# A semaphore wait from each indirect scatter to the eviction of the step ahead of it

## The chip, the cores and the metric

The kernel runs on one core of one Trainium2 chip. The metric is the device time of one execution in microseconds, the median over several runs. In the profile PE is TensorE, PEld its weight loads, DVE is VectorE, ACT is ScalarE, POOL is GpSimd, and SP is SyncE, which issues most of the DMAs. A "q" behind an engine's name means its sequencer.

## The reference

Four sequences of 10048 rows with 128 channels go through a long convolution (by FFT in the reference) with a filter that a small network makes from position embeddings. Each row of the result then goes to one of 16 experts, which are chosen in two stages (a group, then an expert within it).

```python
h_filt = (np.maximum(pos_emb @ w1, 0.0) @ w2) * np.exp(-0.01 * pos)[:, None]
u = x * v
y = np.fft.irfft(np.fft.rfft(u, n=2*S, axis=1) * np.fft.rfft(h_filt, n=2*S, axis=0)[None], n=2*S, axis=1)[:, :S]
a = x * y                                   # 4 x 10048 x 128, then seen as 40192 rows
g = np.argmax(a @ w_group, axis=1)          # group, and its softmax weight
e = np.argmax(a @ w_expert[g], axis=1)      # expert in the group, and its weight
out = g_w * e_w * (np.maximum(a @ moe_w1[g, e], 0.0) @ moe_w2[g, e])
```

## The kernel before

The program has two parts: `conv`, and behind it `moe`. The convolution is a two-step discrete Fourier transform by matmuls. The loop `for b in range(self.nbat + 1)` in `conv` handles one sequence per round, in two phases that follow one another.

**The forward phase** of round b has 43 steps of three channels (GD = 3). A step multiplies x by v (`product`, L434, on DVE, from an `xv` load that SP issues at L431), folds the product into sums and differences (`fold`: L447 on DVE or POOL, L448 on POOL for b > 1), takes the first transform on PE (`dft_blocks`, L387), and evicts it from PSUM into the large buffer `z` (L392, a copy on ACT for every b > 0). `run_ahead` is called first in each step: the product is traced four steps ahead of the transform and the fold three steps ahead. Loads have five buffers (NLOAD), folded products five (NPROD). A load's buffer is free when both halves of its fold are done. For b > 0 the inverse transform of the round before is woven into the same steps: transposes of `z` on PE (`turned`, L648 and L658) with a copy on ACT (tt, L660), then for every second step a group of matmuls (`inverse_blocks`, L683 and L691), two copies on ACT (oo, L700 and L701), and on DVE an addition (yt, L704) and a product (xy, L706) with `xo`, whose load ACT's own queue issues (L671).

**The middle phase** has 40 iterations, two frequencies in each. PE makes `psb` (L458), DVE the products t (L616, L619), POOL sums and differences of these into y (L617, L620), and, four iterations later, PE transforms back (`back`, L628) and ACT evicts into `z` (L635). The last round (b = 4) has only the inverse of the last sequence.

**Routing and scatters.** After a sequence is through, `chosen` and `ranked` pick experts and compute for every row an address among pages of 256 rows, one expert to a page. The rows themselves go there by indirect DMAs of POOL: `put` (L353) scatters one block of 128 rows with 130 columns out of a staged tile (`stg`, which SP loads and whose last two columns POOL fills in at L345), and `clear` (L368) marks the unused rows of pages. They wait in a list, and `scatter(n)` takes up to n of them: one or two in each forward step, after `run_ahead` and before that step's `dft_blocks`; one in three of four middle iterations, behind `back`; one or two in each step of the last round, behind `inverse_blocks`; the rest in `moe`, where `fetch` calls it.

**Order.** A planner orders each engine's instructions by a model of times, with program order as the priority. `keep_in_program_order` ties an instruction behind the one traced before it on its engine, without a semaphore. `between` does that for a scatter and also ties it behind the last instruction passed to `beyond`; `beyond` ties its instruction (L345, L448 for b > 1, L620, the part of L706 on POOL) behind all scatters since. So on POOL a scatter of a forward step stands in front of the next step's L448, and a scatter of a middle iteration in front of the next L620.

Of the kernel before, what the change touches and what calls it, by code (L numbers as in the profile page):

```python
# [139 lines left out]
class Kernel:  # L140
# [5 lines left out]
    def emit(self):  # L146
        tc, nc, d = self.tc, self.nc, self.d
        with ExitStack() as ctx:
            cp = ctx.enter_context(tc.tile_pool(name="const", bufs=1))
            self.ident = cp.tile([128, 128], F32, name="ident")  # L150
            make_identity(nc, self.ident)
            st = ctx.enter_context(tc.tile_pool(name="state", bufs=1))
            self.rem = st.tile([128, NE], F32, name="rem")
            self.cur = st.tile([128, NE], F32, name="cur")
            self.used = st.tile([128, 1], F32, name="used")
            for t in (self.rem, self.cur, self.used):
                nc.vector.memset(t, 0.0)
            pg = self.pages
            pg.epg = st.tile([128, pg.hp], F32, name="epg")
            pg.epgi = [st.tile([1, hi - lo], I32, name=f"epgi{lo}") for lo, hi in pg.parts]  # L160
            pg.count = st.tile([1, 1], I32, name="count")
            nc.vector.memset(pg.epg, 0.0)
            self.entries = ctx.enter_context(tc.tile_pool(name="entries", bufs=2))
            self.empty = st.tile([128, ZR, RW], F32, name="empty")
            nc.vector.memset(self.empty, 0.0)
            nc.vector.memset(self.empty[:, :, 128], BIGID)
            self.units, self.staged, self.tick, self.sent = [], 0, 0, None
            self.all = [Page(self, q) for q in range(pg.n)]
            self.w = [None, None]
            with ExitStack() as right:  # L170
                rout = ExitStack()
                self.rp = rout.enter_context(tc.tile_pool(name="rout", bufs=1, reuse_waits="tile"))
                with ExitStack() as c2:
                    routing = self.conv(c2, right)
                with ExitStack() as c2:
                    self.moe(c2, right, routing)
                rout.close()
# [131 lines left out]
    def scatter(self, n):  # L309
        self.tick += 1  # L310
        for _ in range(min(n, len(self.scatters))):
            b, send, tick, u = self.scatters[0]
            if u:
                self.stage(u.k)

            if tick > self.tick and n < NB:
                break
            self.between(send())
            self.scatters.pop(0)

    def unordered(self, ins, group, *others):
# [57 lines left out]
    def dft_blocks(self, b, eo, d0, n, other=False):  # L379

        nc = self.nc
        pool, tag = (self.psA, "ps") if b not in ("h", 0) or d0 // GD % 2 else (self.psT, "pt")
        ps = pool.tile([128, GD, 2 * NB], F32, tag=tag, name="psa")
        for i in range(n):

            for h, hs in enumerate(HALVES):
                nc.tensor.matmul(  # L387
                    ps[hs, i], eo[:, i, hs], self.fa[:, h], start=True, stop=True
                )
        copy = nc.vector.tensor_copy if other else nc.scalar.copy  # L390

        ins = copy(  # L392
            self.z[:, :NB, :, d0 : d0 + n].rearrange("p k s d -> p (k s) d"),
            ps[:, :n].rearrange("p d c -> p c d"),
        )
        self.in_turn(b, ins)
        self.tc.declare_no_dep(ins.ins, group=f"z{b}", reason="every step has channels of its own")
        self.tc.add_to_no_dep_group(f"z{b}", ins.ins)
# [224 lines left out]
    def back(self, k0, n, bp, y):  # L623

        nc = self.nc
        po = self.psT.tile([128, 2, 2, 128], F32, tag="pt", name="pbp")
        for i in range(n):
            nc.tensor.matmul(  # L628
                po[:, i].rearrange("p s d -> p (s d)"),
                bp[:, i],  # L630
                y[:, i].rearrange("p s d -> p (s d)"),
                start=True,
                stop=True,
            )
        nc.scalar.copy(self.z[:, k0 : k0 + n], po[:, :n])  # L635

    def turned(self, d0, n):

# [25 lines left out]
    def inverse_blocks(self, b, xy, d0, n, tts):  # L664

        nc, d, sp = self.nc, self.d, self.sp
        rows = lambda t: t[:, : n * NB].rearrange("p (t d) -> p t d", d=n)
        xo = sp.tile([128, GI * NB], F32, tag="spec", name="xo", bufs=NSPEC)
        src = d["x_out"][b, :, d0 * NB : (d0 + n) * NB]
        if b < self.nbat - 1:  # L670
            nc.scalar.dma_start(xo[:, : n * NB], src)  # L671
        else:
            self.tc.keep_in_program_order(nc.sync.dma_start(xo[:, : n * NB], src))
        po = self.psO.tile([128, GI, NB], F32, tag="po", name="po")
        c0 = d0 % (2 * GI)

        for c in range(c0, c0 + n):


            if c == c0 or c % 4 == 0:  # L680
                g, m = c // 4, min(4 - c % 4, c0 + n - c)
                for h, hs in enumerate(HALVES):
                    nc.tensor.matmul(  # L683
                        po[hs, c - c0 : c - c0 + m].rearrange("p c t -> p (c t)"),
                        tts[0][:, g, hs],
                        self.fi[:, h, 1 + c % 4 : 1 + c % 4 + m].rearrange("p c t -> p (c t)"),
                        start=c == c0,
                        stop=False,
                    )
            for h, hs in enumerate(HALVES):  # L690
                nc.tensor.matmul(  # L691
                    po[hs, c - c0],
                    tts[1 + c // 4][:, c % 4, hs],
                    self.fi[:, h, 0],
                    start=False,
                    stop=c == c0 + n - 1,
                )
        oo = rows(sp.tile([128, GI * NB], F32, tag="oo", name="oo"))
        by_row = po[:, :n].rearrange("p d t -> p t d")
        nc.scalar.activation(oo[0:64], by_row[64:128], AF.Copy, scale=-1.0)  # L700
        nc.scalar.copy(oo[64:128], by_row[0:64])  # L701
        pool, tag, bufs = (self.ap, "y", NY) if b < self.nbat - 1 else (sp, "yt", 2)
        yt = rows(pool.tile([128, GI * NB], F32, tag=tag, name="yt", bufs=bufs))
        nc.vector.tensor_tensor(yt, by_row, oo, ALU.add)  # L704
        helped = b == self.nbat - 1 and d0 // GI % 2 > 0
        ins = (nc.gpsimd if helped else nc.vector).tensor_tensor(  # L706
            xy[:, :, d0 : d0 + n], yt, rows(xo), ALU.mult
        )
        if helped:
            self.beyond(ins)  # L710
# [311 lines left out]
    def moe(self, ctx, right, routing):  # L1022
        tc, nc = self.tc, self.nc
        pools = [
            right.enter_context(tc.tile_pool(name=n, bufs=b, side="right", reuse_waits="tile"))
            for n, b in (("moe", 2),)
        ]
        self.sp = pools[0]
        self.psx = ctx.enter_context(tc.tile_pool(name="psx", bufs=1, space=PSUM, reuse_waits="tile"))
        self.psh = ctx.enter_context(tc.tile_pool(name="psh", bufs=4, space=PSUM, reuse_waits="tile"))  # L1030
        self.psy = ctx.enter_context(tc.tile_pool(name="psy", bufs=2, space=PSUM, reuse_waits="tile"))
        self.pst = ctx.enter_context(tc.tile_pool(name="pst", bufs=1, space=PSUM, reuse_waits="tile"))
        self.psr = lambda shape, name: self.pst.tile(shape, F32, tag="pt", name=name)
        pg = self.pages
        self.routing, self.fix = routing, tc.keep_in_program_order
        self.outs, self.spare, self.owed, self.part = [], 0.0, 0.0, 0.0
        self.work(self.all[: pg.usual])
        if pg.usual < pg.n:
            count = self.sp.tile([1, 1], I32, tag="ep", name="count", bufs=3)
            tc.keep_in_program_order(nc.vector.tensor_copy(count, pg.count))  # L1040
            count = nc.values_load(count, min_val=0, max_val=pg.n)
            self.rest(count, pg.usual)
# [366 lines left out]
```

## Time and profile before

| | us |
|---|---|
| median of 3 runs | 2088.56 |
| lowest, highest | 2079.05, 2088.92 |
| the profiled execution | 2083.55 |
| its span, first to last instruction | 2081.7 |
| PE busy in the span | 1963.7 |
| POOL busy | 1393.3 |
| mean granted TensorE clock | 0.973 |

The span is the time from the first to the last instruction that the profile shows; the execution's own time has 1.85 us more around it. The convolution takes about the first 1010 us. Its first scatter starts at 448.8 us: rounds b = 0 and 1 have none in front of that. Their forward phases with scatters lie at 487 to 587 us (b = 2) and 737 to 827 us (b = 3), the middle phases behind these at 587 to 684 and 827 to 927 us, and the last round from there to about 1010 us.

### The profile page before, as it was taken

To read this page: it belongs to the slowest core of one execution; us is meant where nothing else is said; L and a number is where in the kernel's file an instruction comes from. 1 tells how busy PE (TensorE), PEld (TensorE's weight loads), DVE (VectorE), ACT (ScalarE), POOL (GpSimd) and SP (SyncE) were. 2 spreads that over 40 slices of the span, in tenths; PEclk is the share of its full clock that TensorE was granted. 3 is DMA by queue.
4 is the path that set the end of the run, shared out by engine and by line. 5 is a ranking of instruction groups with operands and counts; after the bars stand their busy time and mean duration, and the time that the engine had idled before them with its cause. 6 is when DMAs were issued, how large, how long until landed. Compare 5 with 4: busy or idle time off the path is not lost.

```text
span 2081.7 us, 53885 instructions
## 1 busy us (share of the span) xinstructions
PE 1963.7 (94%) x18062; PEld 1803.7 (87%) x18062; DVE 1635.2 (79%) x3451; ACT 1408.2 (68%) x3081; POOL 1393.3 (67%) x1481
## 2 busy tenths in 40 slices
PE   8988999988899788989899999999999999999997
PEld 7867888777787577768699999999999999999997
DVE  5587775797558865696698998889999998888885
ACT  6652376435553355436688788888888888888886
POOL 3157600677889888976457677888888886555554
PEclk9999999998999789999999999999999999999999
DMA  4699866976799567968544455555555544443442
GB/s 136 227 264 257 282 178 189 326 208 176 207 308 297 168 186 223 326 225 278 187 130 138 134 154 151 155 178 171 156 161 155 162 149 131 125 135 120 127 126 66
DMA packets 258719, 388.92 MB, mean 187 GB/s; under 512 B 32679, under 2 KB 132626, under 8 KB 258432
## 3 DMA queue, kind: packets, MB, share of 16 engines
q1 hardware_dynamic: 225024, 318.01, 51.0%
q0 software_dynamic: 23904, 51.83, 7.0%
q10 hardware_dynamic: 9504, 15.54, 2.7%
q8 instruction: 146, 2.39, 0.5%
q14 instruction: 141, 1.16, 0.2%
HBM read 303.24 MB, written 83.04 MB: 186 GB/s over the span
## 4 chain that ended last, share of the span: by engine, by line
PE 66%; POOL 10%; DVE 8%; DMA 7%; issue 6%; ACT 2%; SPq 0%; POOLq 0%; ACTq 0%; DVEq 0%
PE py L1278 7%; PE ph L1259 7%; PE ph L1257 7%; PE py L1276 7%; PE py L1277 7%; PE ph L1258 7%; PE psb L458 4%; PE psa L387 4%; PE pbp L628 3%; POOL prow L353 3%; DMA xv<-xv_in 2%; PE ptm L1290 2%; PE px L1214 2%; PE pt L658 2%; PE po L683 1%
## 5 line engine op out<-in xcount | busy, mean ns | idle before, releaser
L1266 DVE SCALAR_TENSOR_TENSOR hl<-ph,hh 128x512 fp32r<-128x512 f32 x656 | 445.1, 683 | 93.0 <-ACT hh L1265 92.2
L1265 ACT ACTIVATE hh<-ph 128x512 fp32r<-128x512 f32 x656 | 393.8, 600 | 137.9 <-PE ph L1259 75.0
L1302 POOL DMA_INDIRECT out<-os,to x328 | 347.2, 1058 | 91.5 <-issue 71.4
L353 POOL DMA_INDIRECT prow<-stg,adr x316 | 350.4, 1109 | 73.0 <-issue 54.1
L1276 PE MATMUL py<-hh,wh 128*128 128x256 f32 x1312 | 398.5, 304 | 0.0
L1278 PE MATMUL py<-hh,wl 128*128 128x256 f32 x1312 | 373.1, 284 | 5.4 <-POOL wl L1246 5.4
L1257 PE MATMUL ph<-xh,wh 128*128 128x256 f32 x1312 | 373.4, 285 | 4.3 <-ACT wh L1239 2.5
L1259 PE MATMUL ph<-xh,wl 128*128 128x256 f32 x1312 | 373.4, 285 | 0.4 <-DVE wl L1246 0.4
L1258 PE MATMUL ph<-xl,wh 128*128 128x256 f32 x1312 | 372.8, 284 | 0.0
L1277 PE MATMUL py<-hl,wh 128*128 128x256 f32 x1312 | 371.3, 283 | 0.0
L1246 POOL TENSOR_TENSOR wl<-ws,wh 128x512 fp32r<-128x512 f32 x162 | 220.0, 1358 | 201.3 <-ACT wh L1239 200.3
L1278 PEld LDWEIGHTS py<-hh,wl 128*128 128x128 f32 x1312 | 251.3, 192 | 8.2 <-POOL wl L1246 8.2
L1257 PEld LDWEIGHTS ph<-xh,wh 128*128 128x128 f32 x1312 | 252.7, 193 | 5.0 <-ACT wh L1239 2.7
L1259 PEld LDWEIGHTS ph<-xh,wl 128*128 128x128 f32 x1312 | 253.0, 193 | 1.1 <-DVE wl L1246 0.8
L1258 PEld LDWEIGHTS ph<-xl,wh 128*128 128x128 f32 x1312 | 253.1, 193 | 0.1
L1277 PEld LDWEIGHTS py<-hl,wh 128*128 128x128 f32 x1312 | 252.7, 193 | 0.0
L1276 PEld LDWEIGHTS py<-hh,wh 128*128 128x128 f32 x1312 | 251.9, 192 | 0.0
L635 ACT COPY z<-pbp 128x512 f32<-128x512 f32 (+1 forms) x160 | 92.6, 580 | 221.8 <-PE pbp L628 214.9
L1246 DVE TENSOR_TENSOR wl<-mw,wh 128x512 fp32r<-128x512 f32 x328 | 236.6, 722 | 0.0
L617 POOL TENSOR_TENSOR y<-t 128x256 f32<-128x256 f32 (+1 forms) x160 | 120.3, 752 | 158.3 <-DVE t L616 153.0
L458 PE MATMUL psb<-z,bt 128*128 128x256 f32 x790 | 203.0, 389 | 10.5 <-DVE hs L591 3.7
L1239 ACT CAST wh<-mw 128x512 fp32r x328 | 205.7, 628 | 0.0
(232 smaller groups left out, 4367.4 us busy)
## 6 DMA issues: line engine op xcount, KB each, us to landing
ws<-m_w SPq DMA_DIRECT2D x328, 256.0 KB
ht<-hspec SPq DMA_DIRECT2D x156, 256.0 KB
xv<-xv_in SPq DMA_DIRECT2D x131, 288.0 KB
bt<-c_b SPq DMA_DIRECT2D x95, 256.0 KB
xg<-prow SPq DMA_DIRECT2D x164, 130.0 KB
bp<-c_bp SPq DMA_DIRECT2D x76, 256.0 KB
stg<-xyd SPq DMA_DIRECT2D x76, 256.0 KB
xyd<-xy SPq DMA_DIRECT2D x57, 256.0 KB
```

The lines of the kernel that those rows point to most:

```text
L353: ins = self.nc.gpsimd.indirect_dma_start(self.d["prow"], bass.IndirectOffsetOnAxis(ap=u.adr[:, t : t + 1], axis=0), u.rows[:, t - u.t0], ...
L458: nc.tensor.matmul(ps[:, i], bt[:, i], self.z[:, k0 + i], start=True, stop=True,)
L1246: ins = v.tensor_tensor(lo, self.matrix(i, half, self.ed), self.wh[i][half].bitcast(F32), ALU.subtract)
L1257: k.fix(nc.tensor.matmul(ph[:, j], wh, self.xh, start=True, stop=False))
L1258: k.fix(nc.tensor.matmul(ph[:, j], wh, self.xl, start=False, stop=False))
L1259: k.fix(nc.tensor.matmul(ph[:, j], wl, self.xh, start=False, stop=True))
L1265: k.fix(nc.scalar.activation(hh, ph, AF.Relu))
L1266: k.fix(nc.vector.scalar_tensor_tensor(hl, ph, 0.0, hh.bitcast(F32), ALU.max, ALU.subtract))
L1276: k.fix(nc.tensor.matmul(self.py, wh, self.hh[c], start=(c == 0), stop=False))
L1277: k.fix(nc.tensor.matmul(self.py, wh, self.hl[c], start=False, stop=False))
L1278: k.fix(nc.tensor.matmul(self.py, wl, self.hh[c], start=False, stop=(c == NC - 1)))
L1302: ins = k.nc.gpsimd.indirect_dma_start(k.d["out"], bass.IndirectOffsetOnAxis(ap=self.to[:, h : h + 1], axis=0), o[:, h], None, bounds_chec ...
```

## The change

A field `pace` keeps the instruction that evicted last. It is set by the eviction of each forward step (L392), of each `back` (L635), and in the last round by the second copy of each inverse group (L701). Each scatter that `scatter` sends while `pace` is set gets a dependency on it of the class that makes a semaphore wait. In a forward step that is the eviction of the step before, since the scatter is traced before its own step's `dft_blocks`; in a middle iteration it is the eviction of the `back` traced just in front of it; in the last round that of the group just traced. Before `moe` sends scatters, `pace` is set to None, so those get no such wait.

```diff
@@ emit
-            self.units, self.staged, self.tick, self.sent = [], 0, 0, None
+            self.units, self.staged, self.tick, self.sent, self.pace = [], 0, 0, None, None
@@ scatter
-            self.between(send())
+            ins = send()
+            self.between(ins)
+            if self.pace is not None:
+                kind = mybir.DependencyInfo(mybir.DependencyClass.Sync, mybir.DependencyReason.DATA)
+                self.tc.add_manual_dep(ins.ins, self.pace.ins.name, kind, reason="one step at a time")
             self.scatters.pop(0)
@@ dft_blocks
+        self.pace = ins
         self.in_turn(b, ins)
@@ back
-        nc.scalar.copy(self.z[:, k0 : k0 + n], po[:, :n])
+        self.pace = nc.scalar.copy(self.z[:, k0 : k0 + n], po[:, :n])
@@ inverse_blocks
-        nc.scalar.copy(oo[64:128], by_row[0:64])
+        ins = nc.scalar.copy(oo[64:128], by_row[0:64])
+        if b == self.nbat - 1:
+            self.pace = ins
@@ moe
-        self.routing, self.fix = routing, tc.keep_in_program_order
+        self.routing, self.fix, self.pace = routing, tc.keep_in_program_order, None
```

## Rows read from the trace of the kernel before

**Rows 1.** The page: busy time of each engine, its share of the span, and its count of instructions.

```profile
PE 1963.7 (94%) x18062; PEld 1803.7 (87%) x18062; DVE 1635.2 (79%) x3451; ACT 1408.2 (68%) x3081; POOL 1393.3 (67%) x1481
```

**Rows 2.** Busy time of the engines in the four stretches, the two forward phases with scatters first, then the middle phases behind them: from:to, length, busy us and count of each engine, granted clock, share of the DMA engines, GB/s.

```profile
487.00:587.00 100.00, 90.50 (x1286) 79.01 (x1286) 55.71 (x99) 61.70 (x109) 81.62 (x93) 0.95 0.77 211
737.00:827.00 90.00, 81.71 (x1140) 71.36 (x1132) 47.83 (x100) 54.35 (x97) 73.43 (x84) 0.92 0.75 211
587.00:684.00 97.00, 89.61 (x567) 69.95 (x565) 78.80 (x154) 38.46 (x89) 89.40 (x113) 1.00 0.92 307
827.00:927.00 100.00, 91.85 (x571) 72.17 (x569) 79.44 (x169) 39.15 (x90) 91.36 (x117) 0.98 0.82 276
```

**Rows 3.** The chain that ended last within 487 to 587 us: its shares by line.

```profile
by line: issue 28.7%; POOL prow L353 21.9%; POOL eo L448 10.9%; DMA xv<-xv_in 8.0%; PE psa L387 5.2%; DMA prow<-stg,adr 4.6%; PE pt L658 3.2%; PE po L683 2.9%; PE po L691 2.7%; ACT oo L700 1.8%; DVE eo L447 1.8%; DVE xv L434 1.7%; ACT oo L7
```

**Rows 4.** The scatter's line L353: all of its scatters, those of the first forward phase with the semaphore instructions of POOL's sequencer at that line, and those of the second forward phase; count, ns min/median/max, first and last start in us.

```profile
L353 POOL DMA_INDIRECT prow<-stg,adr x316: 966/998/1835, 487.5 to 1706.0; - x158
...
L353 POOL DMA_INDIRECT prow<-stg,adr x50: 966/1004/1656, 487.5 to 585.1; - x50
...
L353 POOLq EVENT_SEMAPHORE  x11: 42/43/43, 507.9 to 578.3; - x11
...
L353 POOL DMA_INDIRECT prow<-stg,adr x46: 966/1000/1814, 738.0 to 823.4; - x46
```

**Rows 5.** The timeline of POOL: start, duration in us, line, and in brackets how long the engine was idle before and who ended that.

```profile
487.55 1.03 POOL L353 DMA_INDIRECT prow<-stg,adr  x1 [0.68 <-POOL stg L345]
...
494.81 0.75 POOL L448 TENSOR_TENSOR eo<-xv 96x192 f32<-96x192 f32 x1 [3.60 <-PE psa L387]
...
537.16 1.65 POOL L353 DMA_INDIRECT prow<-stg,adr  x1 [0.16 <-issue]
...
587.85 0.89 POOL L617 TENSOR_TENSOR y<-t 128x256 f32<-128x256 f32 x1 [1.74 <-DVE t L616]
...
600.31 0.99 POOL L353 DMA_INDIRECT prow<-stg,adr  x1 [0.16 <-issue]
...
797.58 0.61 POOL L448 TENSOR_TENSOR eo<-xv 96x192 f32<-96x192 f32 x1
...
803.53 0.61 POOL L448 TENSOR_TENSOR eo<-xv 96x192 f32<-96x192 f32 x1
...
823.40 0.97 POOL L353 DMA_INDIRECT prow<-stg,adr  x1 [0.30 <-issue]
...
827.88 0.89 POOL L617 TENSOR_TENSOR y<-t 128x256 f32<-128x256 f32 x1 [3.51 <-DVE t L616]
...
927.29 0.99 POOL L353 DMA_INDIRECT prow<-stg,adr  x1 [0.17 <-POOL y L620]
...
937.64 1.37 POOL L706 TENSOR_TENSOR z<-yt,xo 128x474 f32<-128x474 f32 x1 [9.35 <-DVE yt L704]
```

**Rows 6.** The timeline of ACT, in the same columns; the row at 824.27 holds the evictions of the last two steps.

```profile
491.09 0.55 ACT L392 COPY z<-psa 128x474 f32<-128x474 f32 x1
...
522.83 0.56 ACT L700 ACTIVATE oo<-po 64x474 f32<-64x474 f32 x1 [3.78 <-DVE eo L447]
...
593.61 0.58 ACT L635 COPY z<-pbp 128x512 f32<-128x512 f32 x1 [1.97 <-PE pbp L628]
...
824.27 1.01 ACT L392 COPY z<-psa 128x474 f32<-128x474 f32 x2
...
933.75 0.55 ACT L701 COPY oo<-po 64x474 f32<-64x474 f32 x1
```

**Rows 7.** Who waited for whom: us in total, times, longest us. The first three rows are of 487 to 587 us, the last two of 737 to 827 us.

```profile
DVE xv L434 <- DMA xv<-xv_in: 16.4, 12, 2.7
...
PE pt L658 <- ACT tt L660: 9.5, 5, 2.9
...
POOL eo L448 <- PE psa L387: 6.5, 5, 3.6
...
PE pt L658 <- ACT tt L660: 8.3, 4, 3.1
...
POOL eo L448 <- PE psa L387: 3.2, 4, 1.7
```

**Rows 8.** The timeline of DVE, in the same columns.

```profile
518.94 0.71 DVE L434 TENSOR_TENSOR xv<-xv 96x384 f32<-96x384 f32 x1 [2.34 <-DMA xv<-xv_in]
...
521.72 0.64 DVE L706 TENSOR_TENSOR xy<-yt,xo 128x474 f32<-128x474 f32 x1
...
537.30 0.64 DVE L706 TENSOR_TENSOR xy<-yt,xo 128x474 f32<-128x474 f32 x1
...
806.75 0.42 DVE L434 TENSOR_TENSOR xv<-xv 96x256 f32<-96x256 f32 x1 [0.75 <-DMA xv<-xv_in]
```

**Rows 9.** The timeline of PE, in the same columns.

```profile
524.96 0.85 PE L658 MATMUL pt<-ident,z 128*128 128x128 f32 x4 [2.06 <-ACT tt L660]
...
803.91 0.98 PE L387 MATMUL psa<-fa,eo 96*64 96x158 f32 x12
```

**Rows 10.** The timeline of SP's queue, in the same columns.

```profile
804.16 0.31 SPq L431 DMA_DIRECT2D xv<-xv_in  x1
```

**Rows 11.** The product L706 on DVE in the first and in the second forward phase: count, ns min/median/max, first and last start.

```profile
L706 DVE TENSOR_TENSOR xy<-yt,xo x19: 487/642/654, 488.8 to 584.8; 128x474 f32<-128x474 f32 x18, 128x316 f32<-128x316 f32 x1
...
L706 DVE TENSOR_TENSOR xy<-yt,xo x16: 488/642/873, 740.8 to 824.8; 128x474 f32<-128x474 f32 x15, 128x316 f32<-128x316 f32 x1
```

## The prediction

> **What bounds the kernel now.** I read the page first: PE is busy 94% of the span, POOL 67% [rows 1]. An average like that hides the stages, so next come the four stretches of the convolution in which POOL scatters [rows 2]. There POOL is busy 82 of 100, 73 of 90, 89 of 97 and 91 of 100 us. The reader is to see that POOL has almost no room just where the change adds a wait; each scatter costs about 1.00 us of it (median 1.00, longest 1.81 in these phases), and there are 50 and 46 in the two forward phases [rows 4]. The chain of waits in the first of these phases confirms it: the scatter and the fold behind it have 33% of it, the xv loads that the fold sets free 8% [rows 3]. PE is nearly as full, and what it loses there is 9.5 and 8.3 us of waiting for the copy tt on ACT [rows 7].
>
> The decisive view is the pairing of scatters with the evictions they would wait for. I counted both off the loops in the order in which they are traced, and took the start of the k-th scatter and the end of its eviction from the timelines. 204 scatters come while `pace` is set (180 of L353, 24 of L368); the other 136 of the 316 [rows 4], and 8 of L368, fall in `moe` and get nothing.
>
> **The change part by part.**
>
> *Middle phases, 60 scatters.* Here the eviction is over long before. The first pair: eviction 593.61 + 0.58 = 594.19, scatter 600.31, so 6.1 us to spare [rows 5, 6]. Over all 60 the margin is 2.1 us or more. The wait is already met: 0 us. That matters, since POOL is at its fullest here.
>
> *Last round, 33 scatters.* One stands ahead of its eviction: it starts at 927.29, the eviction ends at 933.75 + 0.55 = 934.30, 7.0 us later. POOL's next work starts at 937.64 after 9.35 us of idling [rows 5, 6], so the scatter, moved to 934.4 to 935.4, still fits: 0 us. The others have 1 us or more to spare.
>
> *Forward phases, 111 scatters.* 64 of them start before their eviction ends, by 90.9 us together. The first of the 64 starts at 487.55 against 491.64 (491.09 + 0.55), 4.1 us early; the last at 823.40 against 825.00, where the first of the two copies in the row at 824.27 ends [rows 5, 6]. The 90.9 us don't add up, because POOL works in order: once the first scatter has waited, everything behind it is late too, and the following ones wait only for what is left. I moved POOL's rows accordingly, each only as far as its eviction or its predecessor pushes it, and left the evictions where they are. The folds L448 then come 2.4 us later on average in the first phase and 2.2 us in the second (4.2 and 3.8 us at most). Idle time of POOL, such as the 3.60 us in front of the L448 at 494.81 [rows 5], takes up a part early on.
>
> What is behind a waiting scatter on POOL: the L448 of a step four further on, and by it two consumers. The first is PE's transform. The shortest lead of a finished fold over its transform in either phase behind the first scatters is 797.58 + 0.61 = 798.19 to 803.91, 5.7 us [rows 5, 9]; most are 8 to 12 us. A shift of 2 to 4 us is hidden by that, and would cost its full length if the lead were gone. The second is the load buffer. L448 ends at 804.14 (803.53 + 0.61), SP issues the next xv at 804.16, and DVE, which idled 0.75 us for it, multiplies at 806.75 [rows 5, 8, 10]. So here the shift goes on without cover: DVE's L434 waits longer, and yt and xy stand behind it. How that gets to PE is seen at 519 us: L434 waits 2.34 us for its load, xy comes at 521.72, only then ACT issues an xo load and goes on with oo at 522.83 after 3.78 us of idling, and PE's transposes, whose tt copy stands behind that, start at 524.96 after 2.06 us [rows 6, 8, 9].
>
> Lower end for the forward phases: 0 (DVE's wait for a load falls where nobody waits). Upper end for a shift that happens once in each phase: 2.4 + 2.2 = 4.6 us. I take the upper one: it is nearest to the chain, which runs through the fold and the loads. At the ends of the phases, POOL has 1.74 us idle before 587.85 and 3.51 us before 827.88 [rows 5]; the last scatters, 2.1 us late, leave 0.4 to 0.5 us in the first case and nothing in the second. Together 5.1 us.
>
> *Collisions of POOL with DVE.* A scatter later by 2 us meets other work of DVE. All 12 of the 96 scatters in the two phases that take 1.4 us or more have an L706 over them; the one at 537.16 takes 1.65 us, with the xy product of 0.64 us at 537.30 in it, that is the plain 1.00 and the product's length [rows 5, 8]. There are 35 such products in the two phases [rows 11]. If none met a scatter any more, POOL would gain 12 x 0.64 = 7.7 us; if all did, it would lose 23 x 0.64 = 14.7 us. I take 0, the present mix, and keep both ends. The Trainium skill's page "SBUF — State Buffer", section "Who interferes with whom", says that a VectorE instruction with two SBUF inputs contends with a GpSimd instruction that reads SBUF, but infers that such a tensor_tensor doesn't hold up descriptor generation, which needs the write interface. By that, this term would be 0 at both ends. The 1.65 us row speaks against that inference, so the range keeps both ends.
>
> *The wait itself.* A semaphore instruction of POOL's sequencer takes 0.043 us; 11 of the first phase's 50 scatters have one already [rows 4], and the gap in front of a scatter is the same 0.16 us at 537.16 and at 600.31 [rows 5]. So it fits into that gap: 0 us. If it didn't, 204 x 0.043 = 8.8 us is its upper end.
>
> *The order.* The planner sees the new dependency and may write another order. No row shows one; I bound it by what DVE's order costs now, PE's 9.5 + 8.3 = 17.8 us [rows 7], as a gain or as a loss, and take 0.
>
> Sum: 2083.55 us for the profiled execution, plus 5.1, gives 2088.6. The median of the runs, 2088.56, lies 5.0 us above that execution, so on the median it is 2093.7; I say 2093.
>
> **The rivals.**
>
> *Feedback: slower.* The 5.1 us hold only if PE, made late, doesn't make the evictions late in turn. In the paced state an eviction L392 that follows oo (L700, L701) on ACT releases the scatter at about the time at which DVE, having done yt, starts L706, so every xy product lands on a scatter. For it: the 12 long scatters; POOL has only 6.5 + 3.2 = 9.7 us of waiting for PE in the two phases to take it up [rows 7]. Against it: the loop from an eviction over scatters, fold, load, L434, yt, xy and oo to a later eviction takes about 11 us (two scatters 2.3, fold 0.6, load to L434 2.6 and 0.5, yt and xy 1.3, from xy to the end of oo 2.2, the eviction 0.6, PE about 1 in between; an estimate from rows 5, 6 and 8), and advances six steps; two steps take 96.0 / 18 = 5.3 us by the first phase's xy products [rows 11], six 16 us. Price: 5.1 + 14.7, some 20 us, 2108; it decides once more than 9.7 us of new POOL time arise.
>
> *A better order: faster.* L434 stands ahead of yt and xy of earlier steps in DVE's order, though its load isn't there (16.4 us of waiting in the first phase [rows 7]). If the planner, seeing POOL later, puts L434 behind them, PE's 17.8 us go: 2088.56 + 5.1 - 17.8 = 2075.9. Against it: POOL's own work fills the phases, and they can't shrink by more than its idle time, 9.7 us of which waits for PE.
>
> *Nothing happens: no change.* DVE's longer wait for loads falls where ACT would have waited for PE anyway, and the change costs 0: 2088.6.
>
> **How the numbers follow.** Forecast 0.40, feedback 0.28, a better order 0.17, nothing 0.15. A measurement of this kernel can tell about 0.5% (10.4 us) from no change; its three runs spread over 9.9 us. Faster by more than that is the better order alone: 0.17. Slower is the feedback, and 0.04 of the forecast where a part of the collisions comes with it: 0.32. The rest, 0.51, is within. The range reaches from the price of the better order, 2075, to the feedback's with a little more, 2111; the forecast's own is 2086 to 2100.
>
> **What would show it.** In the changed profile the scatters of the forward phases should start 0.1 us or so behind an L392, with POOL idle before some of them in favour of ACT; in the middle phases there should be no such wait. The lead of L448 over its transform should shrink by 2 to 3 us and stay above 3. If PE's waiting for tt grows by more than 5 us, or the scatters of 1.4 us and more become 25 rather than 12, it is the feedback; if the L434 rows move behind L704 and L706 and PE's waiting falls, the better order. The prediction is wrong if either phase changes its length by more than 6 us, or if the middle phases change at all.

## The result and the profile after

The changed kernel takes 2104.84 us in the median of five runs (2101.66 to 2106.26), the kernel before 2080.74 us in five runs (the three of the table above and two more). The ratio is 1.0091, with a 95% interval of 1.0076 to 1.0107: slower, by about 19 us. The two medians lie 24.1 us apart, more than that: the runs of before fall into two groups (three at 2079.05 to 2080.74, two at 2088.56 and 2088.92), and its median is one of the lower ones. With three runs it was 2088.56. The traces, whose executions took 2083.55 and 2104.84 us, differ by 21.0 us in their spans.

Seven lines were added to the file, so line numbers moved: the scatter L353 is now L357, the eviction L392 is L396, the fold's two lines L447 and L448 are L452 and L453, the product L434 is L439, its load L431 is L436, the issue of xo L671 is L676, oo (L700, L701) is L705 and L706, yt L704 is L711, xy L706 is L713, the transposes L658 and their copy L660 are L663 and L665, psa L387 is L391, the middle phases' eviction L635 is L640, and the stg load L342 is L346.

First the view that sums busy time by stretch, for the same four stretches as [rows 2], two forward phases and then the two middle phases behind them, with its columns:

```profile
487.00:600.00 113.00, 96.39 (x1283) 83.09 (x1278) 54.97 (x101) 60.45 (x109) 82.52 (x96) 0.89 0.67 186
748.00:847.00 99.00, 84.16 (x1144) 72.84 (x1145) 50.50 (x105) 53.62 (x97) 74.53 (x88) 0.90 0.67 189
600.00:696.00 96.00, 89.57 (x566) 70.05 (x565) 77.16 (x154) 38.77 (x89) 89.63 (x114) 0.99 0.93 312
847.00:947.00 100.00, 92.38 (x570) 71.87 (x569) 80.66 (x174) 39.15 (x90) 91.92 (x117) 0.98 0.81 277
```

The middle phases are as long as they were; the forward phases are 113 and 99 us instead of 100 and 90. POOL's busy time in the first one hardly moved (81.62 to 82.52 us), so the time is not work, it is waiting. Evictions serve as landmarks. The timeline of ACT after the change has these, the eviction of step 7 (where the scatters begin) and of the last steps in the first phase, then the first of the middle phase, then the same two of the second forward phase:

```profile
491.20 0.56 ACT L396 COPY z<-psa 128x474 f32<-128x474 f32 x1
...
596.98 1.02 ACT L396 COPY z<-psa 128x474 f32<-128x474 f32 x2
...
606.33 0.59 ACT L640 COPY z<-pbp 128x512 f32<-128x512 f32 x1 [1.97 <-PE pbp L633]
...
732.02 0.56 ACT L396 COPY z<-psa 128x474 f32<-128x474 f32 x1
...
843.77 1.01 ACT L396 COPY z<-psa 128x474 f32<-128x474 f32 x2
```

and that of the kernel before, those that [rows 6] doesn't hold:

```profile
584.24 1.02 ACT L392 COPY z<-psa 128x474 f32<-128x474 f32 x2
...
721.49 0.55 ACT L392 COPY z<-psa 128x474 f32<-128x474 f32 x1
```

The first landmark is late by 0.1 us (491.20 against 491.09), the end of the phase by 12.7, the first row of the middle phase by 12.7 (606.33 against 593.61), the second phase's begin by 10.5, its end by 19.5. The end of the span is late by 21.0. So the loss is 12.6 us in the first forward phase, 9.0 in the second, and in all about nothing elsewhere. It also grows evenly: at steps 14, 21, 28 and 35 of the first phase the evictions end 1.3, 4.4, 8.0 and 10.0 us late.

Who waited for whom in the first forward phase (us in total, times, longest us):

```profile
DVE xv L439 <- DMA xv<-xv_in: 37.1, 22, 3.5
...
PE pt L663 <- ACT tt L665: 16.6, 7, 3.3
ACT oo L705 <- DVE xy L713: 14.0, 4, 4.9
POOL prow L357 <- ACT z L396: 13.3, 12, 2.2
```

The fourth row is the new wait. The first two are those of [rows 7], 16.4 us before and 9.5 us before. PE's share of the loss in this phase can be read off: 5.9 us more busy (90.50 to 96.39, for as many matmuls, while the granted clock of the stretch fell from 0.95 to 0.89) and 7.1 us more waiting for tt make 13 us.

In the second phase it is waiting alone. The view by stretch from the eviction of step 7 to that of step 42, before and after:

```profile
721.49:825.29 103.80, 90.90 (x1244) 78.93 (x1246) 59.69 (x135) 58.98 (x105) 84.27 (x99) 0.88 0.67 188
...
732.02:844.78 112.76, 89.73 (x1244) 77.50 (x1246) 62.84 (x137) 58.16 (x105) 85.37 (x103) 0.89 0.63 175
```

The stretch is 9.0 us longer, while PE's busy time fell by 1.2 us at the same clock. (The table above shows more busy time there only because its two stretches, 737 to 827 and 748 to 847 us, don't begin at the same work: the matmul pe named below starts at 736.21 us before, ahead of the one, and at 749.99 after, within the other.) PE's wait for tt grew from 8.3 [rows 7] to 12.8 us; the routing's matmul pe waited longer for yt, and one transform for an eviction (the first row is of the kernel before, the others of the changed one):

```profile
PE pe L973 <- DVE yt L704: 3.6, 1, 3.6
...
PE pe L980 <- DVE yt L711: 6.6, 1, 6.6
PE psa L391 <- ACT z L396: 2.6, 1, 2.6
```

In the first phase's rows the third one, ACT waiting for xy, names the way the delay travels. The timelines show one turn of it, first POOL,

```profile
524.69 0.99 POOL L357 DMA_INDIRECT prow<-stg,adr  x1 [0.82 <-DVE eo L452]
525.71 1.12 POOL L453 TENSOR_TENSOR eo<-xv 96x192 f32<-96x192 f32 x1
...
532.68 0.99 POOL L357 DMA_INDIRECT prow<-stg,adr  x1 [0.79 <-ACT z L396]
```

then DVE,

```profile
530.33 0.56 DVE L439 TENSOR_TENSOR xv<-xv 96x384 f32<-96x384 f32 x1 [1.33 <-DMA xv<-xv_in]
530.80 0.64 DVE L713 TENSOR_TENSOR xy<-yt,xo 128x474 f32<-128x474 f32 x1
...
542.45 0.64 DVE L713 TENSOR_TENSOR xy<-yt,xo 128x474 f32<-128x474 f32 x1
```

then ACT with its queue ("ACTq"),

```profile
523.68 1.49 ACT L396 COPY z<-psa 128x474 f32<-128x474 f32 x2
...
531.48 0.34 ACTq L676 DMA_DIRECT2D xo<-x_out  x1
531.85 0.56 ACT L396 COPY z<-psa 128x474 f32<-128x474 f32 x1 [1.06 <-DVE xy L713]
...
539.83 0.33 ACTq L676 DMA_DIRECT2D xo<-x_out  x1
540.26 0.56 ACT L705 ACTIVATE oo<-po 64x474 f32<-64x474 f32 x1 [4.96 <-DVE xv L439]
...
541.41 0.55 ACT L396 COPY z<-psa 128x474 f32<-128x474 f32 x1
```

and one row each of SP's queue and of PE.

```profile
526.85 0.31 SPq L436 DMA_DIRECT2D xv<-xv_in  x1
...
542.40 0.86 PE L663 MATMUL pt<-ident,z 128*128 128x128 f32 x4 [3.26 <-ACT tt L665]
```

The eviction of step 17 is the first copy of the row at 523.68 and ends at 524.41. The scatter behind it starts at 524.69. Its row names a DVE fold as the last to be waited for, but it starts 0.28 us behind the eviction's end, as the scatter at 532.68, whose row names ACT, starts 0.27 us behind its own (532.41); so the 13.3 us above leave out some waits that were hit. Behind the scatter stands the fold of step 22, which ends at 526.83. This frees a load buffer; SP issues the load of step 27 at 526.85, and DVE's L439 for it starts at 530.33, after 1.33 us of idling. The xy product stands behind it in DVE's order and ends at 531.44. It frees an xo buffer, for which the issue L676 on ACT's queue has been waiting, and behind that issue stands the eviction of step 20, over at 532.41. The next scatter waited for exactly that. One turn: 8.0 us, three steps further on. The later issue at 539.83 shows the same link with its price: oo had been idle for 4.96 us, and PE's transposes, which need the tt copy behind it, came at 542.40 after 3.26 us.

The phase's pace before the change is 35 steps (7 to 42) in 93.6 us, 2.7 us a step. A loop that takes 8.0 us to advance three steps has that pace already. It has nothing to spare, so each wait that is added inside it is paid again in each turn. That is an argument from rows; the experiments have to show it.

### The profile page after: what moved, and what is told of

It reads as the page before. It is cut to its first block, busy times and chain, and to the rows that moved or that the text cites. A ratio compares the mean times of both kernels' runs of the same rounds, so it can differ in the third digit from the quotient of the medians.

```text
span 2102.7 us, 54018 instructions
## 1 busy us (share of the span) xinstructions
PE 1969.7 (94%) x18062; PEld 1808.6 (86%) x18062; DVE 1627.8 (77%) x3451; ACT 1408.1 (67%) x3081; POOL 1400.1 (67%) x1481
## 4 chain that ended last, share of the span: by engine, by line
PE 74%; DVE 8%; DMA 6%; POOL 6%; issue 3%; ACT 2%; SPq 1%; ACTq 0%; DVEq 0%; POOLq 0%
PE py L1285 7%; PE py L1283 7%; PE py L1284 7%; PE ph L1266 7%; PE ph L1264 7%; PE ph L1265 7%; PE psb L463 6%; PE psa L391 5%; PE pbp L633 5%; DMA xv<-xv_in 3%; PE pt L663 2%; PE po L688 2%; PE po L696 2%; PE ptm L1297 2%; PE px L1221 2%
## 5 line engine op out<-in xcount | busy, mean ns | idle before, releaser
L357 POOL DMA_INDIRECT prow<-stg,adr x316 | 342.6, 1084 | 113.3 <-issue 60.4
L640 ACT COPY z<-pbp 128x512 f32<-128x512 f32 (+1 forms) x160 | 92.7, 580 | 223.2 <-PE pbp L633 213.3
```

What stands on the lines that cost most here:

```text
L357: ins = self.nc.gpsimd.indirect_dma_start(self.d["prow"], bass.IndirectOffsetOnAxis(ap=u.adr[:, t : t + 1], axis=0), u.rows[:, t - u.t0], ...
```

## The experiments

Times are medians; the kernel before ran beside each on the same chip. It took 2082.8 us beside e1 to e4, 2082.5 beside e5 to e7, 2082.6 beside e8 to e10, each of these three groups on a chip of its own.

**e1, the order without the waits.** The planner sees the same dependency, but no semaphore is made.

```diff
-                kind = mybir.DependencyInfo(mybir.DependencyClass.Sync, mybir.DependencyReason.DATA)
+                kind = mybir.DependencyInfo(mybir.DependencyClass.NoSync, mybir.DependencyReason.DATA)
```

> The same dependency, but of the class that makes no semaphore wait: the planner writes nearly the order of the changed kernel (PE, ACT and SP the same, a few rows of DVE and POOL apart), and nothing waits. Theory W (the waits of the forward phases close a loop: eviction, scatter, fold, load, DVE, ACT, PE, eviction): about the time of before, 2080 to 2087 us, and no row in which a scatter waits for z. Theory O (the order that the planner wrote, L447 ahead of yt and xy on DVE and xv loads behind staging loads on SP, costs the time): near the changed kernel, 2097 to 2106.

2083.01 us, ratio 0.9996 (0.9981 to 1.0012). The new order alone (but for a few places on DVE and POOL it is that of the changed kernel) costs nothing; the loss is in the waits.

**e2, the waits without the order.** The waits of the changed kernel, with the order of the kernel before written out as edges without semaphores.

```diff
+    def as_before(self):
+        made = {i.name: i for i in self.nc.cur_bb.bb.instructions}
...
+            for a, b in zip(run, run[1:]):
+                self.tc.add_manual_dep(made[b], a, kind, reason="as before")
```

> The changed kernel with its waits, with the order of the kernel before written out for every engine. Theory W: near the changed kernel, 2097 to 2107 us, the scatters of the forward phases waiting some 25 us for z. Theory O: 2080 to 2088 us.

2114.04 us, ratio 1.0149 (1.0128 to 1.0170), 7 us above the upper end of theory W. The waits by themselves cost 31 us, and the order that the planner found for them gives back 9 (by the medians; 12 by the ratios). Its first forward phase has the same rows, larger (its file is 55 lines longer: L494 is the product, L720 the tt copy, L412 the scatter):

```profile
DVE xv L494 <- DMA xv<-xv_in: 39.3, 23, 3.3
...
PE pt L718 <- ACT tt L720: 19.5, 7, 5.5
POOL prow L412 <- ACT z L451: 15.1, 11, 2.9
```

**e3, no waits in the forward phases.** Those of the middle phases and the last round stay.

```diff
@@ dft_blocks
-        self.pace = ins
+        self.pace = None
```

> The waits of the 111 scatters of the forward phases left out, those of the middle phases and of the last round (93) kept. Theory W: 2079 to 2085 us, since the margins there were 1 us and more, but for one scatter. Theory S (each wait costs by itself, wherever it stands, as a semaphore instruction or a lost head start on POOL): 93 of 204 of the 24 us, some 2092 us.

2085.25 us, ratio 1.0006 (0.9989 to 1.0023). The 60 waits of the middle phases and the 33 of the last round cost nothing that can be measured, as do their semaphore instructions. The planner's order here is that of the kernel before, but for a few places on POOL and SP, so like is compared with like.

**e4, one eviction earlier.** In the forward phases a scatter waits for the step before the one it waited for.

```diff
@@ dft_blocks
-        self.pace = ins
+        self.pace, self.last = self.last, ins
```

> Each scatter of a forward step waits for the eviction of the step before the one that it waits for in the changed kernel; all else as in the changed kernel. Theory W: the loop gets one step (2.7 us) of room, the waits go from 25 us to under 6, and the time to 2082 to 2090 us. If only the number of waits counted, or the order that goes with them: 2097 to 2106 us.

2087.96 us, ratio 1.0021 (1.0006 to 1.0036). One step of slack takes away 17 of the 22 us that the changed kernel's median lies above the 2082.8. The planner wrote another order here too, on DVE nearer to that of the kernel before (14 of 3451 places differ) than to that of the changed kernel (55). That isn't what gains: with the order of the kernel before the waits of the changed kernel cost more, not less (e2). The wait is still in place and is hit eight times in the first phase, but by 3.5 us instead of 13.3:

```profile
DVE xv L439 <- DMA xv<-xv_in: 30.8, 20, 2.6
...
PE pt L663 <- ACT tt L665: 11.8, 5, 2.9
...
POOL prow L357 <- ACT z L396: 3.5, 8, 0.8
```

In its two forward phases 16 scatters take 1.4 us or more, in those of the changed kernel three, in those of the kernel before 12 (counted in POOL's timelines). Of these three the kernel that loses most has the fewest, so the long scatters don't go with the loss.

**e5, the step's own eviction.** The scatters move behind `dft_blocks` and wait for their own step's eviction.

```diff
                     self.run_ahead(b, i, made, folded)
-                    self.scatter(1 + (i >= 12 and i % 2))
                     self.dft_blocks(*folded[i])
+                    self.scatter(1 + (i >= 12 and i % 2))
```

> Each forward step's scatters are sent behind the step's own transform, so that they wait for that step's eviction, one step later than in the changed kernel. Theory W: in the trace of the changed kernel the loop from an eviction over scatter, fold, load, L434, xy, the issue of xo and back to an eviction takes 8.0 to 9.6 us and advances three steps (2.7 to 3.2 us for each, against 2.7 in the kernel before); now it advances two, 4.0 to 4.8 us for each, so over some 75 steps with scatters 75 to 150 us more than the changed kernel: 2180 to 2255 us. Theory C (what the waits cost is a fixed lateness of POOL at the start of each phase, and collisions): one step later costs as much again as the first, 2120 to 2135 us.

2111.22 us, ratio 1.0140 (1.0095 to 1.0185). Both expectations miss: that of the loop (W) by 69 us at the least, the other (C) by 9. The planner, which sees the scatters later, wrote another order: against the changed kernel 60 of DVE's 167 products stand further back, and 14 of SP's issues elsewhere. So this run doesn't test what a later wait costs in an order that stays.

**e6, the folds of rounds 2 and 3 on DVE, with the waits.** If the loop runs through a fold that stands behind a scatter on POOL, taking the fold off POOL opens it. Both halves of a fold are then on DVE; only in the first twelve steps of a round L452 stays on POOL, as it was.

```diff
-        sub = nc.vector if (b or d0 >= FIRST and odd) and b < 2 else nc.gpsimd
+        sub = nc.vector if b or d0 >= FIRST and odd else nc.gpsimd
...
-        self.beyond(ins) if b != "h" and b > 1 else self.in_turn(b, ins)
+        self.in_turn(b, ins)
```

> The changed kernel with the second half of the fold (L448) on DVE instead of POOL for rounds 2 and 3 as well, so that no fold and no load buffer stands behind a waiting scatter. Theory W: the waits of the scatters hurt nobody; within 4 us of the same kernel without the waits (sent with this one). Theory C: still some 20 us above that one.

2067.11 us, ratio 0.9926 (0.9898 to 0.9955): faster than the kernel before, and so than the changed one. The waits are all there and last longer than in the changed kernel; over the whole span its scatters wait

```profile
POOL prow L357 <- ACT z L396: 45.0, 34, 6.9
```

against this row of the changed kernel:

```profile
POOL prow L357 <- ACT z L396: 25.6, 21, 3.4
```

**e7, the same without the waits.** The edit of e6 on the kernel before.

> The kernel before with the second half of the fold on DVE for rounds 2 and 3, without any new wait: what e6 is to be compared with. POOL loses 43 folds of 0.61 us in each of two phases in which it is nearly full, DVE gets 43 of 0.35 us, of which it has the room: 2065 to 2085 us; more than 2090 if DVE, in order, becomes what bounds the phase.

2105.80 us, ratio 1.0118 (1.0083 to 1.0153): slower, where a gain was expected, and not within 4 us of e6 as theory W had it. By these two the waits would gain 39 us. SP's queue shows something else. Rows of e7, SP waiting to issue stg loads until scatters have landed, and DVE waiting for its loads:

```profile
SPq L342 <- DMA prow<-stg,adr: 86.9, 33, 6.4
...
DVE xv L434 <- DMA xv<-xv_in: 89.4, 51, 8.7
```

In e6 the same two rows are

```profile
SPq L346 <- DMA prow<-stg,adr: 5.9, 4, 2.9
...
DVE xv L439 <- DMA xv<-xv_in: 51.6, 49, 4.4
```

In SP's order of e7 the stg loads L342 of a forward phase stand close together, one or two behind every one or two xv loads, where e6 has on average one behind every three; with POOL freed and no dependency on an eviction, the planner seems to take the scatters to go out early. In e7 they do: all 96 of the two forward phases start ahead of the eviction that e6 ties them to, in the median by 40 and 36 us. Such a stg load waits for its buffer until an older scatter has landed, and the xv loads stand behind it.

**e8, e6's dependencies as order only.** e6 with the class NoSync, as in e1.

> e6_fold_on_dve_wait's kernel with the class NoSync: the planner still sees scatter behind eviction, but no semaphore waits. In e7 SP's order puts the stg loads L342 early, and SP's queue waits 86.9 us for scatters to land (5.9 us in e6); here the stg loads stand spread out, as in e6. Theory O (e6 gained and e7 lost by the order alone): 2058 to 2075 us, SP's wait for landings under 20 us. Theory W (the waits themselves gain something, by holding scatters back): 2085 to 2106, the phases about as long as in e7.

2064.04 us, ratio 0.9907 (0.9885 to 0.9930); its interval overlaps that of e6. SP's wait for landings is

```profile
SPq L346 <- DMA prow<-stg,adr: 7.6, 5, 3.4
```

So the order that comes from telling the planner of the dependency carries the whole gain, and the waits themselves cost or gain nothing that can be told once no fold stands behind a scatter. And they are waits that are hit: in e8, where nothing waits, 95 of the 96 scatters start ahead of the eviction that e6 makes them wait for, by 384 us together (58 of 96 in the kernel before, by 88 us). Whether all of e7's loss is SP's order wasn't tried alone; DVE's and POOL's orders differ too.

**e9 and e10, the xo issue off ACT.** The other link of the loop: SP issues the xo load, in the changed kernel (e9) and in the kernel before (e10).

```diff
@@ inverse_blocks
         if b < self.nbat - 1:
-            nc.scalar.dma_start(xo[:, : n * NB], src)
+            nc.sync.dma_start(xo[:, : n * NB], src)
```

> The changed kernel with the xo load L676 issued by SP in place of ACT, so that ACT's queue no longer waits for DVE's xy in front of an eviction. Theory L (the loop eviction, scatters, fold, load, L439, yt and xy, xo issue on ACT, eviction closes through ACT's issue): the forward phases lose most of their growth of 12.6 and 8.9 us against e10, so e9 lies 0 to 7 us above e10. Theory P (the loop closes through PE: late folds, or po freed late by yt): 15 us or more above e10.

> The control of e9: the kernel before with the xo load issued by SP. SP's queue then waits for the xy that frees xo's buffer and holds up the xv loads behind it, so it may be slower than before by itself: 2080 to 2100 us under both theories. What tells is e9 less e10, 0 to 7 us by L, 15 or more by P.

e9 takes 2075.30 us, ratio 0.9962 (0.9942 to 0.9983); e10 2074.08 us, ratio 0.9955 (0.9938 to 0.9972). That e10 is faster than the kernel before was not expected; that e9 lies 0 to 7 us above it was, by theory L. The waits that cost 24 us with the issue on ACT (2104.84 against 2080.74) cost 1.2 us without it, within what can be told from nothing. ACT's waits over the whole span show the link. The changed kernel:

```profile
ACT oo L705 <- DVE xy L713: 27.5, 8, 5.1
...
ACT z L396 <- DVE xy L713: 20.2, 8, 7.2
...
ACT tt L665 <- DVE xy L713: 6.6, 2, 4.6
```

Together 54 us, against 24.5 in the kernel before; e9 and e10 have no such row. And in the first forward phase of e9 (487 to 590 us) the added wait is nearly always met:

```profile
POOL prow L357 <- ACT z L396: 1.5, 5, 0.9
```

While ACT no longer stands behind DVE, DVE still waits for loads there (24.8 us, 18 times). But e9 doesn't test the loop by itself, since its waits have little to wait for: in e10, which has none, 90 of the 96 scatters of the forward phases already start behind the eviction that e9 ties them to, in the median 5.9 and 4.9 us behind (38 of 96 in the kernel before). So what the pair shows is that the scatters run ahead of the evictions only with the issue on ACT's queue. That a wait which is hit returns by this queue rests on the rows of the turn above and on the 54 us; that it costs nothing once the fold is out of its way is what e6 and e8 show.

**e11 and e12, both edits together.** e11 is e8, and e12 is e6, each with the xo load issued by SP.

> e8 with the xo load issued by SP as well: no waits, folds of b > 1 on DVE, ACT without the xo issue. If the two gains add (18.6 us of e8, 8.6 us of e10), 2056 us; DVE, which takes over the folds and is what ACT's issue waited for, may be the bound then, and the sum comes out at 2060 to 2075.

> e11 with the semaphore waits put back. Theory L (a wait is paid only where folds stand behind scatters on POOL and ACT's queue stands behind DVE): within 6 us of e11. Rival (the waits cost by themselves, whatever the links): 12 us or more above e11.

These two ran on another chip, on which the kernel before takes 2143.61 us, 61 us more than beside the others; the part behind the last xy product, which no edit touches, takes 1117 us in the trace of e12 and 1078 in that of the kernel before, so most of them lie there. Only the ratios can be used: e11 1.0018 (0.9975 to 1.0061), e12 0.9958 (0.9929 to 0.9988). On this chip nothing is left of the two gains without the waits. Since neither e8 nor e10 ran on it, this doesn't show that they don't add; they may be missing there singly too. With the waits the kernel is 0.6% the faster, some 13 us, though the two intervals touch. That is more than theory L's 6 us, and the other way from the rival's 12 us above e11, so the rival that waits cost by themselves falls here too: between the start of round 2 and the end of the second forward phase e12's scatters stand waiting for 59 us without a loss.

```profile
POOL prow L357 <- ACT z L396: 59.1, 22, 8.0
```

e11 has in the same stretch, 461 to 849 us in its trace, a wait that e12 has not,

```profile
POOL prow L357 <- DMA stg<-xyd: 74.7, 17, 8.8
```

scatters standing on POOL for a stg load that hasn't come. Why the loads come so late there stays open, as no further run was made on that chip.

The loop could also be opened by more load buffers or a fifth for xo; neither fits into the space that is left, and it wasn't tried.

## Why the prediction was right, and where it was wrong

The forecast was 2093 us, the result is 2104.84 us: inside the range of 2075 to 2111, but the forecast had the kernel within 0.5%, and it is 0.9% slower. The range reaches that far only because of the feedback rival, whose price was worked out for another mechanism than the one that was found, so that it holds the result is luck in part. By the prediction's own sign, "if either phase changes its length by more than 6 us", its account of the forward phases was wrong: they changed by 12.6 and 9.0. On the profiled executions, for which the sum was made, 2088.6 was expected and 2104.84 came: 21.0 us of span where the sum had 5.1.

*Middle phases and last round: right.* The waits there are met. In the middle phase from 612 to 696 us the only wait for an eviction in front of a scatter is

```profile
POOL prow L357 <- ACT z L640: 0.2, 1, 0.2
```

and e3 gives 0. The single scatter that the last round moves, at 927.29 us before [rows 5], now starts at 956.49 us, behind its L706 (955.19 + 0.55 us), at the end of 10.15 us in which POOL is idle.

*The wait itself: right where it is met.* Its price of 0 inside the gap holds there by e3. Where it is hit, the scatter starts 0.27 to 0.28 us behind the eviction's end, not the "0.1 us or so" of the prediction; that is a link of the loop too.

*PE is covered by the lead of the folds: right.* No row of the changed kernel's forward phases has PE waiting for a fold. The way the delay goes on, through L448, the load, L434, xy, the xo issue and oo to PE's transposes, was read correctly from 519 us in the trace of before. Each link is in the rows above.

*"Upper end for a shift that happens once in each phase: 2.4 + 2.2 = 4.6 us": the step that failed.* I moved POOL's rows "and left the evictions where they are". But the way that I had just followed ends on ACT, in whose queue the eviction stands behind oo and the xo issue. A late scatter makes its own release late. What was mis-sized is this term: 12.6 and 9.0 us in place of 2.4 and 2.2 (and the 0.5 at the phases' ends). e4 and e6 with e8 show why: with one step of slack in the loop the shift costs 5 us, and with the fold taken out from behind the scatters nothing that can be told.

*The feedback rival had the price, 2108, and the wrong mechanism.* It put the growth down to xy products that land on scatters. The number of long scatters in the forward phases fell from 12 to 3, and the mean of a scatter in the first one from 1114 to 1053 ns:

```profile
L357 POOL DMA_INDIRECT prow<-stg,adr x50 | 52.7, 1053 | 29.3 <-ACT z L396 13.3 <-issue 8.8 <-DVE eo L452 2.9
```

```profile
L353 POOL DMA_INDIRECT prow<-stg,adr x50 | 55.7, 1114 | 10.7 <-issue 7.4 <-POOL stg L345 2.6 <-DVE xv L434 0.3
```

(changed kernel, then the kernel before; busy us and mean ns of one, then the idle time in front.) Collisions gave 3.0 us back there. The count behind the 14.7 us was wrong as well: it took the 23 products without a long scatter as meeting none, but 29 of the 96 scatters before have an xy over a part of them, 17 of which take less than 1.4 us. Against the rival I had set the loop's length: "takes about 11 us", "and advances six steps". The duration was 3 us too long (the turn that I followed above takes 8.0 us), the advance twice what it is: three steps. I had counted the five load buffers forward and not what DVE's order takes back: the product of step 27 stands ahead of the xy that lets ACT evict step 20. With three steps the estimate would have said 11 us against 8.0 of pace, and the loop decides; with six it looked as if it had 5 us to spare.

*"What would show it" told the right case.* PE's wait for tt was to grow by more than 5 us if it fed back: it grew by 7.1 and 4.5, more than that in the two together. The long scatters were offered as a second sign, and contradicted the mechanism. The chain of the first phase says the same: the scatter's share fell from 21.9% [rows 3] to 6.9%, the loads' rose from 8.0% to 13.7%.

```profile
by line: PE psa L391 16.4%; DMA xv<-xv_in 13.7%; issue 10.3%; PE po L688 8.9%; PE po L696 8.6%; POOL prow L357 6.9%; POOL eo L453 6.5%; PE pt L663 5.7%; ACT oo L706 3.2%; DVE eo L452 3.2%; ACT z L396 2.8%; DVE xv L439 2.8%; DVE xy L713 2.1%
```

*The order: taken as 0, between -17.8 and 17.8 us.* By e1 it is 0 without the waits; by e2 and the result it is worth -9 us with them (-12 by the ratios). The better-order rival had that sign, but its own sign, L434 behind xy, didn't come.

## What to carry to other kernels

Before a wait is priced by moving one engine's rows, follow the delay until it meets the thing that is waited for; if it does, price the loop: its time for one turn, over the steps that it advances in the orders as they stand, against the pace. If that is no faster than the pace, each wait inside is paid again in every turn, and one step of slack, or one link less, is worth nearly all of it. A wait of an engine that nothing stands behind may last long and cost nothing (45 us in e6).

## What was not expected of the hardware

*An issue that waits holds up its engine.* The xo issue L676 takes 0.33 us of ACT's queue, yet moving it to SP made the kernel before 8.5 us faster (e10), with the same bytes. The Trainium skill's page "DMA: Bandwidth & Descriptors", section "Issuing engines are not separate DMA queues", says that issuing from several engines saves only the time of the issue on the sequencer, which is usually small beside the DMA itself. The 0.33 us bear that out. What the section doesn't speak of is the wait in front of the issue, up to 5.1 us in the row "ACT oo L705" above, which the engine's compute instructions share: 24.5 us in all in the kernel before, and none in e10. The 66 issues that moved are 22 us of ACT's queue by themselves; which part of the 8.5 us is theirs wasn't separated.

*Long scatters and xy.* An overlap alone doesn't make a scatter long; where the product begins does. In the two forward phases of the kernel before 29 of 96 scatters have an xy product over a part of them. In twelve of these the product starts between 0.02 us ahead of the scatter's start and 0.15 us behind it, and eleven of the twelve take 1.4 us or more; of the other 17 one does. After the change 26 scatters have such a product, and three are long. It isn't the only cause: four of the 13 long ones of e10 have no xy over them. One of the three that are left shows it again: 1.72 us, with the product of 542.45 in it.

```profile
542.24 1.72 POOL L357 DMA_INDIRECT prow<-stg,adr  x1 [0.51 <-DVE yt L711]
```

*The clock.* In the lengthened first forward phase the granted clock was 0.89 on average instead of 0.95, a mix of its levels of 1.2 and 2.4 GHz, while PE's waits grew. PE's 5.9 us of added busy time came with it. How much of that phase's loss is the clock's own wasn't separated. The loss doesn't need it: from step 7 to step 42 of the second phase the granted clock was 0.88 before and 0.89 after, and 9.0 us were lost.
